# An instruction list laid out anew: attention and gated convolution FFN on one core, 852 entries, same work, another order

## The chip, the cores and the metric

The kernel runs on one core of one Trainium2 chip. The metric is device time in microseconds (us), the median of several executions. Before the change it is 177.59 us, over three runs that lie between 177.56 and 177.61 us.

## The reference

A linear attention without softmax is followed by a gated convolution network. Batch 8, 8 heads, 576 positions, head size 64, so 512 model columns; 1024 hidden columns.

```python
kv  = einsum('bhsd,bhse->bhde', k, v)
out = einsum('bhsd,bhde->bhse', q, kv)
x   = out / sqrt(mean(out*out, axis=-1) + 1e-6) * g_norm     # then (batch, 576, 512)
h   = maximum(x @ w_in, 0.0)                                 # 512 -> 1024
conv_out[s] = sum over k of conv_w[k] * h[s + k - 1]         # 3 taps along the positions
y   = (h * sigmoid(conv_out)) @ w_out                        # 1024 -> 512
```

## The kernel before

All inputs are read in float32 and turned into bf16 by the loads; the result goes back in float32. The eight batches are worked on in pairs for the last matmul, and otherwise one by one.

What each engine does, and when, is written in one string, `ORDER`. Each entry is a short name with its arguments, and a last loop at the end of the kernel calls one small function for each entry and then ties every engine's instructions to exactly the order in which they were issued. So the list is the schedule: an engine takes its instructions in the order of the list, and waits at the first one whose operands or target are not ready. Behind an `@` stands which of several equal buffers the entry writes: one of the eight banks of matmul results (two banks for entries that need a pair), one of the row buffers for output, one of the buffers for q, k, v, x, or one of the two sets of tap buffers. An entry that takes a buffer waits until everybody who read its previous content is done, a transfer out included.

The entries of which this text speaks, with the line of their work in the profile (arguments: batch, then half or tile):

- `Lq`, `Lk`, `Lv` (L347): load of q, k or v of one batch, issued by GpSimd (POOL).
- `qt` (L433) transposes q on TensorE, `qd` (L443, VectorE) copies it out. For batches 6 and 7 `tq` (L467) has the transfer engines transpose it, issued by SyncE (SP).
- `kv`, `kz` (L402, L479): k times v; `kvd` (L414, VectorE) or `kva` (L416, ScalarE) copies it out. `kx` (L489): a copy with halves swapped, by transfer.
- `ot`, `ox` (L460, L500): q times kv. `sq` (L509, ScalarE) squares it, `oc` (L521, ScalarE) copies it out.
- Normalisation, batches 0 to 3: `on` or `oq` (L528 with a full array, L537 with four 64-row pieces) sums the squares, `nl` (L545, ScalarE) takes the inverse root, `mo` (L556, VectorE) makes x.
- Normalisation, batches 4, 5 and 6, 7 together: `ss` (L566), `ln` (L574, ScalarE), `sl` (L581 to L584, four VectorE instructions), then `sp` (L593) spreads the result over the rows and `mu` (L599, VectorE) makes x.
- `hk`, `hs`, `hm` (L658, L628, L613): x times w_in; `rh`, `re` (L640, L619, ScalarE): the maximum with 0, which makes h.
- The convolution: `ta` (L681 and L682, VectorE) multiplies h by two of the taps, `aa` (L687) and `ab` (L692) add; `sg` (L698, ScalarE) is the sigmoid, `mg` (L722, VectorE) multiplies it into h.
- The last matmul: `om` (L732) in groups of four matmuls, two groups to a tile of 128 rows; the last tile in two halves, `oh` (L757). `ea` (L738, ScalarE) or `ed` (L743, VectorE) copies a tile out to a row buffer, `eh` (L767) or `dh` (L772) a half; `st` (L748) and `sh` (L777) store it, issued by SP.

ScalarE has two sets of functions, one for the inverse root and one for the sigmoid. A change from one to the other is an instruction of its own (L227, `ACT_TABLE_LOAD`), which `nl`, `ln`, `sc` and `sg` place when the other set is in.

Of the kernel before, what the change touches and what calls it, by code (L numbers as in the profile page):

```python
# [64 lines left out]
sq.0.1.1@3 oq.0.0.1@0 nl.0.0.1@2 fi.1.512@4 fi.1.512@4 hk.0.1.0.0@4 hk.0.1.0.1 rp.1.0@0 on.0.1.1@0 nl.0.1.1@3
hk.0.2.0.0@5 hk.0.2.0.1 rp.2.0 dg.3 mo.0.0.1 dg.2 hk.0.3.0.0@4 hk.0.3.0.1 hk.0.0.0.0@2 hk.0.0.0.1 rp.0.0 hk.0.0.1.0@3
rp.3.0 hk.0.1.1.0@5 hk.0.3.1.0@0 mo.0.1.1 hk.0.3.1.1 rp.3.1 hk.0.1.1.1 rp.1.1 hk.0.0.1.1 rp.0.1 dg.0 hk.0.2.1.0@1
hk.0.2.1.1 qt.1.0.0@6 kv.1.0.1@4 rp.2.1 cv.0.2@2 sc.0.2@0 cv.0.3@0 qd.1.0.0@2 kvd.1.0.1@1 ot.1.0.1@6 sc.0.3 pl
sq.1.0.1@4 cv.0.1@4 cv.0.0@2 Lq.1.2.2 Lk.1.2.2 Lv.1.2.2 sc.0.1@1 fi.2.512@0 qt.1.1.0@0 qd.1.1.0@3 mg.0.1.1 Lo.0.8
sc.0.0 mg.0.1.0 oq.1.0.1@4 nl.1.0.1@4 mo.1.0.1@1 fi.1.512@2 hk.0.5.1.0@2 hk.0.5.0.0@3 hk.0.5.0.1 rp.5.0 hk.0.5.1.1  # L70
rp.5.1 ta.0.1.5@0 hk.0.4.1.0@0 hk.0.4.1.1 rp.4.1 hk.0.7.0.0@1 hk.0.7.0.1 kv.1.1.1@4 kvd.1.1.1 rp.7.0 ot.1.0.0@2
sq.1.0.0@5 hk.0.7.1.0@6 hk.0.7.1.1 rp.7.1 ta.0.1.7@1 ot.1.1.1@0 sq.1.1.1@6 oq.1.0.0@4 nl.1.0.0@5 mo.1.0.0 hk.0.4.0.0@6
hk.0.4.0.1 rp.4.0 hk.0.6.1.0@7 hk.0.6.1.1 rp.6.1 oq.1.1.1@4 nl.1.1.1@6 mo.1.1.1 hk.0.6.0.0@6 Lq.2.0.4@2 hk.0.6.0.1
rp.6.0 ta.0.1.4 hk.1.6.1.0@7 ta.0.1.6 hk.1.0.1.0@2 ot.1.1.0@4 sq.1.1.0@7 aa.0.1.2 hk.1.1.1.0@3 hk.1.2.1.0@6 hk.1.6.1.1
# [5 lines left out]
Lq.3.0.4@0 Lk.3.0.4@0 Lv.3.0.4@1 Lq.4.0.4@1 aa.1.1.0 hk.1.4.0.0@3 om.0.1.0.4@2 rh.1.4.1 hk.1.4.0.1 rh.1.4.0  # L80
om.0.2.0.4@5 kv.2.0.2@6 mg.0.1.3 om.0.1.4.4 ab.1.1.0 sg.1.1.0 sg.1.1.1 kvd.2.0.2@2 ot.2.0.1@0 sq.2.0.1@0 ed.0.1@0
st.0.1 qt.3.1.0@6 qd.3.1.0@1 Lk.4.0.4@1 Lv.4.0.4@0 Lq.5.0.4@2 om.0.2.4.4 on.2.0.1@2 qt.3.0.0@6 qd.3.0.0@2 nl.2.0.1@8
mo.2.0.1@2 om.0.3.0.4@4 ea.0.2@1 ot.2.1.1@6 ot.2.1.0@2 mg.1.1.0 om.0.3.4.4 ed.0.3@2 sq.2.1.0@1 sq.2.1.1@2 on.2.1.0@0
nl.2.1.0@9 mo.2.1.0 om.0.0.0.4@5 hk.1.3.0.0@4 on.2.1.1@0 st.0.2 nl.2.1.1@0 mo.2.1.1 om.0.0.4.4 ed.0.0@3 ot.2.0.0@2
sq.2.0.0@3 hk.1.3.0.1 rh.1.3.0 st.0.0 kv.3.0.2@0 kvd.3.0.2@0 on.2.0.0@6 nl.2.0.0@1 mo.2.0.0 hs.2.0.1@4 rh.2.0.1@1
hs.2.5.1@5 rh.2.5.1 ot.3.1.1@0 sq.3.1.1@4 ta.1.1.5@1 ot.3.0.1@6 sq.3.0.1@5 hs.2.1.1@4 rh.2.1.1 hs.2.4.0@5 rh.2.4.0
ta.1.1.4 ta.1.1.2@0 pn hs.2.4.1@2 rh.2.4.1 hs.2.1.0@3 rh.2.1.0 on.3.1.1@4 nl.3.1.1@2 hs.2.2.0@2 rh.2.2.0 hs.2.5.0@3
rh.2.5.0 on.3.0.1@4 nl.3.0.1@3 aa.1.1.2 mo.3.1.1@0 hs.2.2.1@2 rh.2.2.1 hs.2.0.0@3 rh.2.0.0 ot.3.0.0@0 sq.3.0.0@6
mo.3.0.1 qt.4.0.0@4 qd.4.0.0@3 ta.1.1.3 ab.1.1.2 aa.1.1.1 ot.3.1.0@2 sq.3.1.0@7 hs.2.3.1@6 rh.2.3.1 on.3.0.0@4
nl.3.0.0@4 hs.3.4.1@7 rh.3.4.1 hs.3.1.1@6 rh.3.1.1 on.3.1.0@4 nl.3.1.0@5 mo.3.0.0 hs.3.6.1@7 rh.3.6.1 hs.2.6.0@6  # L90
mo.3.1.0 qt.5.0.0@4 qd.5.0.0@0 ab.1.1.1 qt.4.1.0@0 qd.4.1.0@4 sg.1.1.5 sg.1.1.4 Lq.6.0.4@0 mg.1.1.2 ta.1.1.6@1
ta.1.1.7 aa.1.1.3 hs.2.3.0@7 rh.2.3.0 hs.3.0.1@2 rh.3.0.1 rh.2.6.0 sg.1.1.3 sg.1.1.2 hs.3.7.0@3 hs.3.2.0@4 rh.3.2.0
hs.3.3.0@5 rh.3.3.0 rh.3.7.0 kv.4.0.2@0 kvd.4.0.2@1 hs.3.0.0@2 hs.3.3.1@6 mg.1.1.1 Lk.5.0.4@0 rh.3.3.1 hs.3.2.1@7
rh.3.2.1 hs.3.7.1@4 rh.3.7.1 hs.3.6.0@5 rh.3.6.0 rh.3.0.0 ab.1.1.3 ta.2.2.2@0 ta.2.2.3 hs.3.4.0@3 rh.3.4.0 sg.1.1.7
hs.3.1.0@4 hs.3.5.0@5 sg.1.1.6 rh.3.1.0 qt.5.1.0@0 qd.5.1.0@2 ot.4.0.0@6 sq.4.0.0@0 mg.1.1.3 rh.3.5.0 om.0.7.0.4@2
Lv.5.0.4@1 Lq.7.0.4@1 Lk.6.0.4@1 oc.4.0.0@6 hs.2.7.1@3 rh.2.7.1 ot.4.0.1@0 sq.4.0.1@1 oc.4.0.1@7 kv.5.0.2@4 ta.2.2.0@1
kvd.5.0.2@2 ot.4.1.0@6 oc.4.1.0@8 om.0.7.4.4 aa.2.2.1 ta.2.2.1 ed.0.7@4 aa.2.2.0 ot.5.0.0@4 sq.4.1.0@2 sq.5.0.0@3
oc.5.0.0@9 ot.5.0.1@0 sq.5.0.1@4 om.0.8.0.4@3 om.0.8.4.4 ed.0.8@5 ab.2.2.1 ot.5.1.1@6 oc.5.0.1@0 sq.5.1.1@5 ot.4.1.1@4
sq.4.1.1@6 oc.4.1.1@1 om.0.5.0.4@2 om.0.5.4.4 ed.0.5@0 ab.2.2.0 ot.5.1.0@0 om.0.4.0.4@3 ss.4.4.2@4 sq.5.1.0@7 ss.5.4.2
# [725 lines left out]
```

## Time and profile before

| | before |
|---|---|
| median time of three runs | 177.59 us (177.56 to 177.61) |
| span of the profiled execution, first to last instruction | 175.6 us |
| instructions | 5070 |
| TensorE matmul busy | 167.9 us (96%), 2097 recorded |
| VectorE busy | 149.5 us (85%) |
| ScalarE busy | 148.9 us (85%) |
| GpSimd busy | 22.2 us (13%) |
| granted TensorE clock | 1.000 |

No time of its own is recorded for the profiled execution; its span is 2.0 us under the median, and that is what lies around the span. On TensorE, instructions overlap: a matmul of 512 columns has a duration of 379 ns in the records while they start about 0.22 us apart. So TensorE's busy share says little, and the times from one start to the next are read instead. A few matmul records are missing (2097 of 2114 are there).

### The profile page before, as it was taken

How to read it: one execution, taken by the hardware profiler on the slowest of the kernel's cores; microseconds unless marked ns; L12 is line 12 of the kernel's file. 1: busy time of each engine (PE TensorE's matmuls, PEld its weight loads, DVE VectorE, ACT ScalarE, POOL GpSimd, SP SyncE). 2: the span in 40 equal slices, each digit the busy share in tenths (PEclk: the TensorE clock that was granted, in tenths of full speed). 3: DMA queues.
4: the chain of work that ended last, by engine and by line, in shares of the span. 5: the costliest groups of instructions: out<-in, count | busy, mean ns of one | idle time of the engine just before them, and what ended most of it. 6: DMA issues, size and time to landing. Idle time of an engine off the chain costs nothing.

```text
span 175.6 us, 5070 instructions
## 1 busy us (share of the span) xinstructions
PE 167.9 (96%) x2097; PEld 100.0 (57%) x2114; DVE 149.5 (85%) x290; ACT 148.9 (85%) x268; POOL 22.2 (13%) x35
## 2 busy tenths in 40 slices
PE   7979999999999999999999999999999999999992
PEld 2334766676447677644467764444877744444451
DVE  2796638899688899999999998989999999999950
ACT  2368899999978999999999998999999967676721
POOL 3094512200603013030000000000000000000000
PEclk9999999999999999999999999999999999999999
DMA  5999999999999999999999050330310003064486
GB/s 159 392 323 207 207 207 207 208 208 209 207 241 230 227 207 207 170 182 197 258 181 161 14 134 0 119 123 0 119 63 0 0 0 116 13 239 175 179 304 237
DMA packets 25911, 29.11 MB, mean 166 GB/s; under 512 B 6036, under 2 KB 20384, under 8 KB 25888
## 3 DMA queue, kind: packets, MB, share of 16 engines
q0 software_dynamic: 13296, 14.50, 49.2%
q1 hardware_dynamic: 12048, 13.11, 26.2%
q10 hardware_dynamic: 544, 1.18, 1.7%
q8 instruction: 16, 0.26, 0.6%
q14 instruction: 7, 0.06, 0.1%
HBM read 32.52 MB, written 9.44 MB: 239 GB/s over the span
## 4 chain that ended last, share of the span: by engine, by line
PE 76%; DVE 12%; ACT 5%; DMA 3%; issue 3%; ACTq 0%; DVEq 0%
PE banks L732 32%; PE banks L628 14%; PE banks L613 9%; PE banks L658 4%; DMA stg<-in_v_dram 3%; PE banks L460 3%; DVE h L722 2%; PE banks L708 2%; ACT taps L698 2%; PE banks L402 2%; PE banks L593 2%; PE banks L433 1%; PE banks L528 1%; DVE taps L681 1%; PE banks L286 1%
## 5 line engine op out<-in xcount | busy, mean ns | idle before, releaser
L732 PE MATMUL banks<-w_out_sb,h 128*128 128x512 bf16 x267 | 62.8, 379 | 1.2 <-issue 0.6
L698 ACT ACTIVATE taps<-taps,cw 128x576 bf16<-128x576 bf16 (+1 forms) x44 | 40.6, 958 | 5.7 <-DVE taps L692 5.5
L732 PEld LDWEIGHTS <-h 128*128 128x128 bf16 x280 | 26.2, 98 | 30.0 <-issue 1.1
L628 PE MATMUL banks<-x,w_in_sb 128*128 128x288 bf16 (+2 forms) x256 | 34.2, 286 | 0.0
L640 ACT ACTIVATE h<-banks 128x288 bf16<-128x288 f32 (+2 forms) x80 | 29.5, 460 | 0.3 <-PE banks L658 0.2
L628 PEld LDWEIGHTS <-w_in_sb 128*128 128x128 bf16 x256 | 24.4, 98 | 7.8 <-issue 0.8
L722 DVE TENSOR_TENSOR h<-h,taps 128x1152 bf16<-128x1152 bf16 (+1 forms) x24 | 22.8, 952 | 1.2 <-ACT taps L698 1.2
L687 DVE TENSOR_TENSOR taps<-taps 128x1152 bf16<-128x1152 bf16 (+1 forms) x22 | 21.5, 978 | 0.5
L509 ACT ACTIVATE sq<-banks 128x576 bf16<-128x576 f32 (+2 forms) x32 | 20.8, 691 | 1.1 <-PE banks L460 1.1
L692 DVE TENSOR_TENSOR taps<-taps,h 128x1152 bf16<-128x1152 bf16 (+1 forms) x22 | 21.4, 972 | 0.3
L681 DVE TENSOR_SCALAR taps<-h,cw 128x576 bf16<-128x576 bf16 (+1 forms) x44 | 18.7, 424 | 0.6 <-ACT h L665 0.5
L682 DVE TENSOR_SCALAR taps<-h,cw 128x576 bf16<-128x576 bf16 (+1 forms) x44 | 18.4, 418 | 0.0
L738 ACT ACTIVATE row<-banks 128x512 f32<-128x512 f32 x23 | 13.5, 597 | 5.7 <-PE banks L732 4.2
L658 PE MATMUL banks<-x,w_in_sb 128*128 128x288 bf16 (+2 forms) x128 | 17.7, 286 | 0.1
L613 PE MATMUL banks<-x,w_in_sb 128*128 128x288 bf16 x128 | 16.9, 286 | 0.0
L556 DVE SCALAR_TENSOR_TENSOR x<-banks,cw,rs 128x576 bf16<-128x576 f32 (+2 forms) x16 | 13.0, 816 | 3.9 <-ACT rs L545 3.6
L658 PEld LDWEIGHTS <-w_in_sb 128*128 128x128 bf16 x128 | 12.0, 98 | 4.4 <-issue 0.5
L227 ACT ACT_TABLE_LOAD x10 | 12.8, 1283 | 2.0 <-issue 1.8
L613 PEld LDWEIGHTS <-w_in_sb 128*128 128x128 bf16 x128 | 12.3, 98 | 3.7 <-issue 0.2
L443 DVE COPY qT<-banks 128x1152 bf16<-128x1152 bf16 (+2 forms) x13 | 8.8, 681 | 5.7 <-PE banks L433 5.7
L545 ACT ACTIVATE rs<-banks,eps_sb 128x576 f32<-128x576 f32 (+2 forms) x16 | 11.8, 740 | 1.1 <-PE banks L528 1.1
L599 DVE SCALAR_TENSOR_TENSOR x<-o,cw,banks 128x576 bf16<-128x576 f32 (+2 forms) x16 | 12.1, 810 | 0.7 <-PE banks L593 0.5
(89 smaller groups left out, 162.9 us busy)
## 6 DMA issues: line engine op xcount, KB each, us to landing
out_dram<-row SPq DMA_DIRECT2D x35, 256.0 KB, 2.3
q_sb<-in_q_dram POOLq DMA_DIRECT2D x6, 576.0 KB, 17.9
k_sb<-in_k_dram POOLq DMA_DIRECT2D x6, 576.0 KB, 14.5
v_sb<-in_v_dram POOLq DMA_DIRECT2D x6, 576.0 KB, 17.9
stg<-in_v_dram ACTq DMA_DIRECT2D x2, 576.0 KB, 6.2
stg<-in_k_dram SPq DMA_DIRECT2D x4, 288.0 KB, 6.9
w_in_sb<-in_moe_w_in_dram POOLq DMA_DIRECT2D x2, 512.0 KB, 9.9
w_out_sb<-in_moe_w_out_dram POOLq DMA_DIRECT2D x1, 1024.0 KB, 15.5
```

The lines of the kernel that those rows point to most:

```text
L509: nc.scalar.activation(T["sq", b, u, s], T["o", b, u, s], AX.Square)
L613: nc.tensor.matmul(ps[:, s, :HS], w_in_sb[:, t, f * P:(f + 1) * P], T["x", b][:, t, c0:c1], start=(t == 0), stop=(t == NT - 1))
L628: nc.tensor.matmul(ps, w_in_sb[:, t, f * P:(f + 1) * P], T["x", b][:, t, c0:c1], start=(t == 0), stop=(t == NT - 1))
L640: nc.scalar.activation(h, fr, AX.Relu)
L658: nc.tensor.matmul(T[at], w_in_sb[:, t, f * P:(f + 1) * P], T["x", b][:, t, c0:c1], start=(t == 0), stop=(t == NT - 1))
L681: nc.vector.tensor_scalar_mul(tap[:, 0, f % 2, :n, 8:8 + S], h[:, f], cw[:, f:f + 1])
L682: nc.vector.tensor_scalar_mul(tap[:, 1, f % 2, :n, :S], h[:, f], cw[:, 2 * NF + f:2 * NF + f + 1])
L687: nc.vector.tensor_add(tap[:, 1, :, :n, :S], tap[:, 0, :, :n, 7:7 + S], tap[:, 1, :, :n, 1:1 + S])
L692: nc.vector.tensor_add(y, y, span(b, n)[:, 2 * j:2 * j + 2])
L698: nc.scalar.activation(y, y, AX.Sigmoid, scale=cw[:, NF + f:NF + f + 1])
L722: nc.vector.tensor_mul(h, h, tap_of(b, j)[:, 1, :, :n, :S])
L732: nc.tensor.matmul(T["om", p, m], h[:, f, m * P:(m + 1) * P], w_out_sb[:, f, :], start=(f == 0), stop=(f == NF - 1))
```

## The change

The string `ORDER` is written anew. It has 852 entries before and after, and no function of the kernel changes. Nearly all entries are the same in another order; a few are exchanged for one that does the same on another engine or in another shape:

- `kvd.2.0.2` and `kvd.3.0.2` (VectorE) become `kva` (ScalarE);
- of the copies of output tiles, `ea.1.8`, `ea.3.1` and `ea.3.5` move to VectorE, `ed.2.8`, `ed.3.0`, `ed.3.2`, `ed.3.3` and `ed.3.4` to ScalarE, and the half tile `eh.3.8.0` to VectorE (`dh.3.8.0`);
- `oq.1.1.1` becomes `on.1.1.1`, so there are 2112 matmuls and no longer 2114.

Buffer numbers behind the `@` change as well. Entries of different engines stand in another order to each other from the first line on, but on the engines themselves the order is the same up to a point: TensorE's first difference is at its 453rd matmul, VectorE's at its 73rd instruction, ScalarE's at its 47th, GpSimd's when the load of batch 4 or 5 is reached. In the trace these are at 30 to 35 us.

The last lines of the list, before (two) and after (four):

```diff
-ed.3.7@4 om.3.5.4.4 ea.3.5@3 st.3.5 om.3.4.4.4 ed.3.4@5 st.3.4 st.3.7 om.3.6.4.4 ea.3.6@0 st.3.6 oh.3.8.1@1 eh.3.8.1@2
-sh.3.8.1 oh.3.8.0@0 eh.3.8.0@1 sh.3.8.0
+ab.7.1.2 ta.7.1.6@1 ta.7.1.7 aa.7.1.3 ab.7.1.3 om.3.2.0.4@1 sg.7.1.5 om.3.2.4.4 sg.7.1.4 ea.3.2@1 om.3.1.0.4@0
+om.3.1.4.4 ed.3.1@3 st.3.0 st.3.3 st.3.2 st.3.1 mg.7.1.2 om.3.6.0.4@1 sg.7.1.7 om.3.5.0.4@2 om.3.4.0.4@0 om.3.7.0.4@3
+sg.7.1.6 mg.7.1.3 om.3.4.4.4 om.3.7.4.4 ea.3.4@0 ed.3.7@1 st.3.7 om.3.5.4.4 ed.3.5@2 st.3.4 st.3.5 oh.3.8.0@0
+dh.3.8.0@3 sh.3.8.0 om.3.6.4.4 ea.3.6@4 st.3.6 oh.3.8.1@0 eh.3.8.1@0 sh.3.8.1
```

The first place is VectorE behind the `mg` of the first group of batch 1's convolution, in the trace the stretch from 42.5 to 54.3 us. `taps_72` and `taps_73` are the two tap buffers; L556 is `mo`, L443 is `qd`, L743 is `ed`, L414 is `kvd`. Before:

```order
L692 TENSOR_TENSOR taps_72<-taps_72,h 128x2x576
L414 CAST kvb<-banks 128x256
L743 COPY row<-banks 128x512
L443 COPY qT<-banks 128x1152 x2
L556 SCALAR_TENSOR_TENSOR x<-banks,cw,rs 128x2x288
L722 TENSOR_TENSOR h<-h,taps_72 128x2x576
L743 COPY row<-banks 128x512
L556 SCALAR_TENSOR_TENSOR x<-banks,cw,rs 128x2x288 x2
```

And now:

```order
L692 TENSOR_TENSOR taps_72<-taps_72,h 128x2x576
L681 TENSOR_SCALAR taps_73<-h,cw 128x576
L682 TENSOR_SCALAR taps_73<-h,cw 128x576
L681 TENSOR_SCALAR taps_73<-h,cw 128x576
L682 TENSOR_SCALAR taps_73<-h,cw 128x576
L743 COPY row<-banks 128x512
L443 COPY qT<-banks 128x1152
L687 TENSOR_TENSOR taps_73<-taps_73 128x2x576
L443 COPY qT<-banks 128x1152
L556 SCALAR_TENSOR_TENSOR x<-banks,cw,rs 128x2x288
L722 TENSOR_TENSOR h<-h,taps_72 128x2x576
```

The `kvd` has gone, and two `ta` and an `aa` of the next group have come in between the copies and the `mo`; an `ab` and two more `ta` follow behind the rows shown, again between `mo` instructions. Before, all of these stood behind the last `mo` of batch 2.

The second place is ScalarE around the first `ln` (L574), in the trace from 80.6 to 88.5 us: the last `sq` of batches 4 and 5 (L509), two changes of the function set (L227), the `oc` (L521), `ea` (L738), `sg` (L698) and `rh` (L640). Before:

```order
L509 ACTIVATE sq<-banks 128x2x288
L227 ACT_TABLE_LOAD
L574 ACTIVATE rs<-banks,eps_sb 128x320
L521 ACTIVATE o_1919<-banks 128x2x288
L521 ACTIVATE o_1921<-banks 128x2x288
L640 ACTIVATE h<-banks 128x288
L738 ACTIVATE row<-banks 128x512
L227 ACT_TABLE_LOAD
L698 ACTIVATE taps_72<-taps_72,cw 128x2x576
L738 ACTIVATE row<-banks 128x512
L640 ACTIVATE h<-banks 128x288 x2
```

And now:

```order
L640 ACTIVATE h<-banks 128x288
L521 ACTIVATE o_1866<-banks 128x2x288
L509 ACTIVATE sq<-banks 128x2x288 x3
L227 ACT_TABLE_LOAD
L574 ACTIVATE rs<-banks,eps_sb 128x320
L521 ACTIVATE o_1999<-banks 128x2x288
L521 ACTIVATE o_2009<-banks 128x2x288
L738 ACTIVATE row<-banks 128x512
L227 ACT_TABLE_LOAD
L698 ACTIVATE taps_72<-taps_72,cw 128x2x576
L738 ACTIVATE row<-banks 128x512
L640 ACTIVATE h<-banks 128x288 x2
```

The `rh` (`rh.2.7.0`) that stood between the two changes of the function set now stands ahead of both.

The third place is the end of SP's queue, the stores of the last tiles. The numbers are those of the row tiles; the last one, `row_3014` before and `row_3012` now, is the half tile that the kernel stores last. Before:

```order
L748 DMA out_0_dram<-row_2984 128x512
L748 DMA out_0_dram<-row_2971 128x512
L748 DMA out_0_dram<-row_2992 128x512
L777 DMA out_0_dram<-row_3003 128x256
L777 DMA out_0_dram<-row_3014 128x256
```

And now:

```order
L748 DMA out_0_dram<-row_2973 128x512
L748 DMA out_0_dram<-row_2982 128x512
L777 DMA out_0_dram<-row_2994 128x256
L748 DMA out_0_dram<-row_3001 128x512
L777 DMA out_0_dram<-row_3012 128x256
```

The first half tile is stored ahead of the last whole one. `row_2973` is `ea.3.4@0`, and the last half tile is `eh.3.8.1@0`: both lie in row buffer 0, so the copy of the last half tile now waits for the store of tile 3.4, which stands behind the store of tile 3.7 on SP.

More of the change, by code (lines that the diff above doesn't have):

```diff
@@ L65 @@
[L65 to L74, printed above, removed]
@@ L80 @@
[L80 to L89, printed above, removed]
@@ L90 @@
[L90 to L99, printed above, removed]
@@ new lines @@
+fi.4.512@1 gt.k.1.0 Li.0.4 pg cad.k.1.0 kv.0.0.1@4 Lq.1.0.2@1 pc Lk.1.0.2@0 kva.0.0.1@0 caa.q.1.0 ot.0.0.0@6
+fi.2.512@0 cad.v.3.0 Lv.1.0.2@1 sq.0.0.0@0 cad.k.2.0 qt.0.1.0@2 caa.v.2.0 Li.4.4 oq.0.0.0@4 fi.2.512@0 cad.k.3.0
+nl.0.0.0@0 qd.0.1.0@1 dg.1 kv.0.1.1@0 fi.2.512@2 Lq.1.2.2 cad.q.0.1 kva.0.1.1 Lk.1.2.2 ot.0.1.0@4 mo.0.0.0@0
+qt.0.0.1@2 fi.2.512@0 sq.0.1.0@1 Lv.1.2.2 cad.q.1.1 qa.0.0.1 oq.0.1.0@0 qt.0.1.1@6 nl.0.1.0@1 ot.0.0.1@2 qd.0.1.1
+sq.0.0.1@2 mo.0.1.0 ot.0.1.1@6 fi.1.512@0 sq.0.1.1@3 oq.0.0.1@0 fi.1.512@4 fi.1.512@4 dg.3 nl.0.0.1@2 hk.0.1.0.0@4
@@ new lines @@
+Lo.0.8 hk.0.1.0.1 mo.0.0.1 on.0.1.1@0 rp.1.0@0 hk.0.2.0.0@5 Lq.2.0.4@2 hk.0.2.0.1 nl.0.1.1@3 hk.0.3.0.0@4 dg.2
+hk.0.3.0.1 hk.0.0.0.0@2 rp.2.0 mo.0.1.1 hk.0.0.0.1 hk.0.0.1.0@3 rp.0.0 hk.0.1.1.0@5 Lk.2.0.4@1 rp.3.0 dg.0
+hk.0.3.1.0@0 hk.0.3.1.1 hk.0.1.1.1 rp.3.1 hk.0.0.1.1 hk.0.2.1.0@1 rp.1.1 Lv.2.0.4@0 hk.0.2.1.1 rp.0.1 qt.1.0.0@6
+rp.2.1 kv.1.0.1@4 qd.1.0.0@2 cv.0.2@2 kvd.1.0.1@1 pl cv.0.3@0 sc.0.2@0 ot.1.0.1@6 Lq.3.0.4@0 sc.0.3 cv.0.1@4
+sq.1.0.1@4 cv.0.0@2 fi.2.512@0 sc.0.1@1 sc.0.0 qt.1.1.0@0 oq.1.0.1@4 fi.1.512@2 qd.1.1.0@3 hk.0.5.1.0@2 hk.0.5.0.0@3
```

104 lines of the change are left out of this document (61 added, 43 removed).

## The prediction

> **What bounds the kernel now.** I read the page first, then the busy time by stretches, the chain of work that ended last, and the timeline where TensorE's starts lie further apart than its work. The page:
>
> ```profile
> span 175.6 us, 5070 instructions
> ## 1 busy us (share of the span) xinstructions
> PE 167.9 (96%) x2097; PEld 100.0 (57%) x2114; DVE 149.5 (85%) x290; ACT 148.9 (85%) x268; POOL 22.2 (13%) x35
> ```
>
> The busy time of each engine by stretches, cut where the program changes its work (convolution and attention of batches 1 to 3, up to the first `ln`, the first `sp`, and so on to the last `mg`):
>
> ```profile
> 33.00:55.00 22.00, 21.63 (x427) 13.71 (x429) 18.69 (x32) 19.82 (x39) 4.46 (x6) 1.00 1.20 218
> 55.00:81.00 26.00, 25.75 (x469) 16.83 (x470) 25.16 (x50) 25.90 (x56) 3.70 (x5) 1.00 1.23 199
> 81.00:91.00 10.00, 9.76 (x146) 5.24 (x147) 9.31 (x15) 9.94 (x16) 0.00 (x0) 1.00 1.25 234
> 91.00:114.00 23.00, 22.79 (x242) 14.67 (x246) 22.09 (x30) 22.51 (x36) 0.00 (x0) 1.00 0.47 86
> 114.00:123.00 9.00, 8.77 (x62) 3.73 (x63) 8.13 (x13) 8.94 (x12) 0.00 (x0) 1.00 0.16 60
> 123.00:141.00 18.00, 18.00 (x149) 14.04 (x148) 17.55 (x24) 17.86 (x37) 0.00 (x0) 1.00 0.12 45
> 141.00:166.70 25.70, 25.54 (x118) 11.59 (x119) 25.32 (x54) 17.92 (x31) 0.00 (x0) 1.00 0.33 123
> ```
>
> The columns are the stretch, its length, and busy time with count of TensorE, its weight loads, VectorE, ScalarE and GpSimd, then clock, transfer share and GB/s. TensorE is busy nearly throughout at full clock, and VectorE and ScalarE are close behind it; only VectorE from 33 to 55 us has much room, 3.3 us of 22. The end of the chain:
>
> ```profile
> 162.94 7.50 PE banks L732 x34
> 170.44 1.76 PE banks L757 x16
> 172.27 0.38 ACT row L767
> ```
>
> 34 matmuls of 512 columns in 7.50 us are 0.221 us each, with no room between them; 16 of half the width take 1.76. So from the first `om` of batches 4 and 5 the run is TensorE streaming to its last matmul, and then one copy, one store and the end. The list can't shorten that stream: both lists hold the same matmuls (but for `oq.1.1.1`, four small ones against two large). What can be won is the time in which TensorE waits. What can be lost has no such limit: any entry that comes late for TensorE is paid in full, as there is no idle time behind it in which to catch up.
>
> **The change part by part.** Up to about 33 us each engine's order is the old one, so nothing is won or lost there. After that I go from wait to wait.
>
> *The wait at `on.3.0.0`.* One row of the table of waits:
>
> ```profile
> PEld L528 <- DVE qT L443: 0.3, 1, 0.3
> ```
>
> TensorE waits 0.3 us for `qd.4.0.0`, whose source lies in the bank that `on.3.0.0` wants. In the new list the two still stand in this order on the same bank, but with one more small `ot` ahead on TensorE, and VectorE comes to the `qd` with less behind it. Won: between 0 and 0.3, I take 0.1.
>
> *The first `sp` and `mu`.* TensorE's timeline, start and duration first, each row a group of equal matmuls:
>
> ```profile
> 86.33 0.42 PE L593 MATMUL banks<-wparts,spread 32*128 32x288 bf16 x4
> 86.67 1.15 PE L628 MATMUL banks<-x,w_in_sb 128*128 128x288 bf16 x8
> 87.84 0.33 PE L500 MATMUL banks<-qT,kvb 64*64 64x320 bf16 x4
> 88.10 0.82 PE L593 MATMUL banks<-wparts,spread 32*128 32x288 bf16 x4
> ```
>
> Four `sp` matmuls take 0.42 when nothing holds them and 0.82 at 88.10: 0.40 of waiting. The eight of `hs` last 1.15 with the overlap of about 0.16 at their end (0.379 of duration against 0.221 from start to start), so `ox` could start at 87.66 and starts at 87.84: 0.18 more. Those at 88.10 want the banks of `hs.2.6.1` and `hs.3.5.1`, which ScalarE's `rh` empties late, since it comes from here:
>
> ```profile
> 84.01 0.42 ACT L640 ACTIVATE h<-banks 128x288 bf16<-128x288 f32 x1
> 84.30 0.62 ACT L738 ACTIVATE row<-banks 128x512 f32<-128x512 f32 x1
> 84.94 1.28 ACT L227 ACT_TABLE_LOAD   x1
> ```
>
> The first of these is `rh.2.7.0`, which the new list has moved ahead of `ln`. It goes from 84.01 to the next start at 84.30, so what follows it on ScalarE is 0.29 earlier, and the `rh` for which `sp` waits are too. Ahead of `ln` ScalarE pays the same 0.29, but there it had last waited for `ot.5.1.0`, which now comes two places sooner on TensorE. I take 0.3 of the 0.40 as won, and another 0.1 because `kvd.6` no longer stands between `sl` and a late `kz`: 0.4 in all. At best both waits go (0.6), at worst the early `rh` holds up `ln` by its 0.29 and nothing is won (a loss of 0.3).
>
> *The second `sp` and `mu`.* TensorE, and then VectorE at the `sl` ahead of it:
>
> ```profile
> 118.22 0.42 PE L593 MATMUL banks<-wparts,spread 32*128 32x256 bf16 x6
> 118.58 1.90 PE L732 MATMUL banks<-w_out_sb,h 128*128 128x512 bf16 x8
> 120.41 0.74 PE L593 MATMUL banks<-wparts,spread 32*128 32x320 bf16 x6
> ```
>
> ```profile
> 116.30 0.33 DVE L581 CAST hi<-rs 128x320 bf16<-128x320 f32 x1 [0.28 <-ACT rs L574]
> ```
>
> The same kind of group takes 0.42 and then 0.74: 0.32 of waiting for a `mu` to free a bank. The new list spreads these six `sp` over three places with half a tile of `om` between, where each bank's `mu` is one earlier; I count that two of three such waits go and one of about 0.2 stays. `sl` itself waits 0.28 for `ln`. ScalarE has one `ea` less ahead of it (0.48 from start to start), but VectorE has that copy more, 0.69 at most. These about cancel. Won: 0.1, between 0.5 won and 0.3 lost.
>
> A switch of the array between 128-row matmuls and smaller ones is not free: eight matmuls from 118.58 to 120.41 are 1.83, and 8 x 0.221 is 1.77, so 0.06 for the switch. The new list has 63 such switches from the first difference on, the old one 62, which changes the sum by 0.06 at most, and I leave it out. The Trainium skill, TensorEngine Tiling, section Key Properties, says that changing the tiling mode drains TensorE; by that the new list is dearer by one drain, and the trace agrees that there is one, and that it is small.
>
> *VectorE from 42 to 56 us.* Who VectorE waits for there, in total, times and longest, and some of its rows:
>
> ```profile
> DVE x L556 <- ACT rs L545: 1.5, 3, 0.7
> DVE qT L443 <- PE banks L433: 0.9, 1, 0.9
> DVE row L743 <- PE banks L732: 0.5, 1, 0.5
> ```
>
> ```profile
> 41.84 0.76 DVE L687 TENSOR_TENSOR taps<-taps 128x1152 bf16<-128x1152 bf16 x1
> 42.52 0.76 DVE L722 TENSOR_TENSOR h<-h,taps 128x1152 bf16<-128x1152 bf16 x1
> ...
> 54.33 0.82 DVE L556 SCALAR_TENSOR_TENSOR x<-banks,cw,rs 128x576 bf16<-128x576 f32 x1 [0.67 <-ACT rs L545]
> 55.06 0.36 DVE L681 TENSOR_SCALAR taps<-h,cw 128x576 bf16<-128x576 bf16 x1
> 55.34 0.36 DVE L682 TENSOR_SCALAR taps<-h,cw 128x576 bf16<-128x576 bf16 x1
> ```
>
> VectorE waits 2.9 us here. Into this the new list puts four `ta` (two instructions of 0.28 each, so 0.56) and an `aa` and an `ab` of 0.68 (from 41.84 to 42.52): 4 x 0.56 + 2 x 0.68 = 3.6 us. Out of it go two `kvd`, whose cost is bounded by the rows here as 0.28 to 0.68 each, say 0.7 together. So 3.6 us of work meet 2.9 + 0.7 = 3.6 us of room. It fits only if each piece falls into its own gap. Following the rows of the new list with these durations I find `mo.2.1.0` and `mo.2.1.1` about 0.25 later than before, with 0.15 to 0.2 of room at the matmuls that wait for their banks (`ot.2.0.0`, `on.2.0.0`). Lost: 0.1, and up to 1.2 where two pieces of 0.6 miss their gaps. What is won, VectorE being ahead by as much later, is worth nothing by itself, since TensorE sets the pace. ScalarE's two `kva` fall where it waited for `on`.
>
> *The end.* The store rows, and the last copies:
>
> ```profile
> DMA to landing us min/median/max: 2.0/2.3/7.8
> ```
>
> ```profile
> 171.35 0.38 ACT L767 ACTIVATE row<-banks 128x256 f32<-128x256 f32 x1 [0.28 <-DMA out_dram<-row]
> 171.76 1.25 SPq L777 DMA_DIRECT2D out_dram<-row  x2
> 172.27 0.38 ACT L767 ACTIVATE row<-banks 128x256 f32<-128x256 f32 x1 [0.54 <-PE banks L757]
> ```
>
> The last copy starts at 172.27, when its matmuls are done. In the new list it also needs row buffer 0 back, that is the landing of the store of tile 3.4. Counted back from 172.27 at 0.221 a matmul: behind tile 3.7 come four matmuls of 3.5, four of 3.6 and 16 halves, 8 x 0.221 + 1.76 = 3.5 us, so tile 3.7 is done at 168.7, its VectorE copy (0.69) at 169.4, and its store is issued then; that of 3.4 follows on SP about 0.4 later, at 169.8. With 2.3 us it lands at 172.1, with 2.7 at 172.5. So the last copy waits for 0 to 0.3 us, and everything behind it with it: lost 0.1. [...]
>
> The loads stand in almost the same order on GpSimd and are the same bytes. Up to the last load of batch 5 the same set has gone through, so `kv.5.0.2` finds its data when it did; v and k of batch 6 come one load earlier.
>
> **The sum.** Won 0.1 + 0.4 + 0.1 = 0.6, lost 0.1 + 0.1 = 0.2: 0.4 less. The span would be 175.2, and with the 2.0 us that lie around it the time is 177.2 (177.59 - 0.4). A measurement of this kernel can tell about 0.2%, 0.36 us, from no change, so this is only just outside.
>
> **The rivals.** *The waits only change their place.* The three gains rest on orders in which ScalarE, VectorE and TensorE hand each other banks with 0.1 to 0.2 us to spare, and a wait that goes at 88 us may return at 90 behind `mu.5`. For it speaks that ScalarE is 9.94 busy of 10 there; against it that the cause of the largest, `rh.2.7.0`, has clearly moved. Then 0.6 shrinks to 0.2, and with 0.2 lost the time is 177.6.
>
> *VectorE misses its gaps.* Between 42 and 56 us two inserted pieces of about 0.6 come ahead of `mo.2.1.0` and `mo.2.1.1` whose `nl` is done already. TensorE's next `ot` and `on` wait for the bank, ScalarE's `nl` waits for `on`, and the delay goes round once to the next `mo`. It decides at 0.15 us: a `mo.2.1.1` that ends later than that against TensorE's stream is paid. For it speaks 3.6 us of work in 3.6 of room; against it that in the new list the pieces do stand behind entries that waited. The price is up to 1.2 on the 177.2: 178.4. Half of it, with the worst of the first `ln` (0.3), gives the same side, 178.1.
>
> That the change doesn't do what it says is excluded by the order of the instructions; what its pricing is worth the rows can't say.
>
> **How the numbers follow.** The forecast, faster by over 0.2%, has 0.44: its gains have named causes. The waits that change their place, within 0.2%, have 0.23. Slower by over 0.2% has 0.33, nearly all the VectorE case, as three engines at 94 to 99% leave little to absorb an error. The gains can't exceed the waits: 0.3 + 0.58 + 0.32 + 0.28 are 1.5, so 176.1 is the floor; taking two thirds of it as the most that is likely, 1.0, the low end is 176.6. The high end is the VectorE case in full, 178.4. Under 2 in 10 lie outside.
>
> **What would show it.** Right: `ox.6.0.0` and the `sp` behind it follow `hs.3.5.1` within 0.3 us of waiting in all; ScalarE's second change of the function set starts 0.3 to 0.6 earlier than 84.94; TensorE's waits at the second `sp` are under 0.25; the last L767 copy waits for TensorE or by 0.1 for the store. Wrong: an `ot` or `on` between 50 and 55 us that waits over 0.2 for L556; a late `ln`; or the last L767 copy released by the store of L748 at 0.3 or more.

## The result, and the profile after

| | before | after |
|---|---|---|
| median of seven runs | 177.57 us (177.48 to 177.63) | 178.05 us (177.95 to 178.15) |
| span of the profiled execution | 175.6 us | 176.3 us |
| `hm.4.7` starts | 88.86 | 88.92 |
| `om.1.3` starts | 121.08 | 121.14 |
| `om.2.1` starts | 140.92 | 140.87 |
| last matmul starts | 171.91 | 172.02 |
| last copy (L767) starts | 172.27 | 173.02 |

The ratio is 1.0027 (95% interval 1.0017 to 1.0038): slower by 0.48 us, where 0.4 less was forecast; inside the range, on the wrong side. The two profiled spans lie further apart, by 0.78 before rounding: the new list was profiled in the slowest of its seven runs (178.15), and around the span the new list spends 1.75 to 1.85 us, the old one 1.90 to 2.01 (from the time and the span of every run on record).

The rows of the table from `hm.4.7` to the last matmul are entries ahead of which TensorE has done the same work in both lists (but for `oq.1.1.1`), so their difference is what the new list has lost or won up to there. 0.05 of each is there at 29 us already, ahead of the first changed instruction. So TensorE's stream is even within 0.1, and the loss lies behind its last matmul. The page:

```profile
span 176.3 us, 5070 instructions
PE 169.7 (96%) x2112; PEld 99.8 (57%) x2112; DVE 148.0 (84%) x287; ACT 150.2 (85%) x271; POOL 22.4 (13%) x35
```

The end: the chain's last row, then ScalarE's last copies, then SP's queue at the stores of tiles 3.7 and 3.4, and the waits on SP and at the end:

```profile
170.44 2.48 DMA out_dram<-row
```

```profile
168.04 0.60 ACT L738 ACTIVATE row<-banks 128x512 f32<-128x512 f32 x1 [2.84 <-issue]
171.46 0.60 ACT L738 ACTIVATE row<-banks 128x512 f32<-128x512 f32 x1 [2.82 <-PE banks L732]
173.02 0.38 ACT L767 ACTIVATE row<-banks 128x256 f32<-128x256 f32 x1 [0.96 <-DMA out_dram<-row]
```

```profile
169.58 0.33 SPq L748 DMA_DIRECT2D out_dram<-row  x1
...
170.44 0.33 SPq L748 DMA_DIRECT2D out_dram<-row  x1
```

Before, the chain ended in 16 half matmuls and the last copy waited for them. Now it ends in a store. Tile 3.4 is copied out by 168.64, but its store stands on SP behind that of 3.7, which goes out at 169.58, and follows only at 170.44. It lands 2.48 later, at 172.91, and the last copy, whose matmuls were done for it at about 172.37 (in the run below with the store moved it starts then), starts at 173.02: 0.65 lost. A last copy that the store releases with 0.3 or more of waiting is a sign of being wrong that the prediction had named.

On the way TensorE's waits changed their place. At the normalisation of batch 3, `on` (L528):

```profile
60.78 0.42 PE L528 MATMUL banks<-sq,ones 128*128 128x288 bf16 x2
61.04 1.14 PE L628 MATMUL banks<-x,w_in_sb 128*128 128x288 bf16 x8
62.25 0.41 PE L528 MATMUL banks<-sq,ones 128*128 128x288 bf16 x2
62.55 1.14 PE L628 MATMUL banks<-x,w_in_sb 128*128 128x288 bf16 x8
```

The idle time ahead of the weights of `on.3.0.0` is 0.16 instead of 0.34, still ended by VectorE's `qd.4.0.0`. But the eight `hs` matmuls from 61.04 are done at 62.02 (8 x 0.122), and `on.3.1.0` starts only at 62.25: it takes the bank of `on.3.0.0`, which ScalarE's `nl` reads until 62.20. In the old list the matmuls behind it started at 62.50, here at 62.55: nothing won.

The first `sp` and `mu`, and what comes ahead of them, TensorE:

```profile
73.69 0.40 PE L460 MATMUL banks<-qT,kvb 64*64 64x288 bf16 x4
73.99 0.77 PE L402 MATMUL banks<-v_sb,k_sb 64*64 64x64 bf16 x72
74.83 0.32 PE L460 MATMUL banks<-qT,kvb 64*64 64x288 bf16 x4
75.08 1.04 PE L732 MATMUL banks<-w_out_sb,h 128*128 128x512 bf16 x4
...
85.42 0.30 PE L593 MATMUL banks<-wparts,spread 32*128 32x288 bf16 x4
85.65 1.04 PE L732 MATMUL banks<-w_out_sb,h 128*128 128x512 bf16 x4
86.62 0.38 PE L593 MATMUL banks<-wparts,spread 32*128 32x288 bf16 x4
86.93 1.15 PE L628 MATMUL banks<-x,w_in_sb 128*128 128x288 bf16 x8
88.16 0.33 PE L500 MATMUL banks<-qT,kvb 64*64 64x320 bf16 x4
88.42 0.57 PE L593 MATMUL banks<-wparts,spread 32*128 32x288 bf16 x4
88.92 1.15 PE L613 MATMUL banks<-x,w_in_sb 128*128 128x288 bf16 x8
90.00 0.42 PE L593 MATMUL banks<-wparts,spread 32*128 32x288 bf16 x4
```

The four groups of `sp` take 0.30 + 0.38 + 0.57 + 0.42 = 1.67 instead of 2.08 (0.42, 0.42, 0.82, 0.42): the 0.4 that the prediction looked for is won here. But TensorE comes to them later, since it has waited more before. One such place is the `ot` and `kv` at 74 us: the stretch from 73.69 to 75.08 is 1.39, and in the old list 1.13, from 73.62 to 74.75 (the recorded start of the `om` behind it less one matmul of 0.22 that is missing in the records), by these rows of before:

```profile
73.62 0.32 PE L460 MATMUL banks<-qT,kvb 64*64 64x288 bf16 x4
73.77 0.92 PE L402 MATMUL banks<-v_sb,k_sb 64*64 64x64 bf16 x72
74.50 0.31 PE L460 MATMUL banks<-qT,kvb 64*64 64x288 bf16 x4
74.97 0.81 PE L732 MATMUL banks<-w_out_sb,h 128*128 128x512 bf16 x3 [0.16 <-issue]
```

And ScalarE's `ln` starts at 82.89 instead of 82.53. Its second change of the function set starts at 85.00 instead of 84.94, where the prediction looked for 0.3 to 0.6 earlier. So `hm.4.7` is where it was. ScalarE had no room to give, as the busy times of the new list by stretches show (ScalarE's is the fourth of the five engines):

```profile
72.00:76.00 4.00, 3.93 (x95) 2.21 (x93) 4.00 (x10) 4.00 (x11) 0.91 (x1) 1.00 0.89 152
76.00:82.00 6.00, 6.00 (x58) 2.64 (x58) 5.80 (x7) 5.98 (x12) 0.76 (x2) 1.00 1.19 225
82.00:86.00 4.00, 4.00 (x90) 1.88 (x90) 3.68 (x8) 3.97 (x6) 0.00 (x0) 1.00 1.19 237
```

### The profile page after: what moved, and what is told of

The parts are those of the page before. It is cut to its first block, busy times and chain, and to the rows that moved or that the text cites. A ratio compares the mean times of both kernels' runs of the same rounds, so it can differ in the third digit from the quotient of the medians.

```text
span 176.3 us, 5070 instructions
## 1 busy us (share of the span) xinstructions
PE 169.7 (96%) x2112; PEld 99.8 (57%) x2112; DVE 148.0 (84%) x287; ACT 150.2 (85%) x271; POOL 22.4 (13%) x35
## 4 chain that ended last, share of the span: by engine, by line
PE 79%; DVE 9%; ACT 5%; DMA 4%; issue 2%; SPq 0%; ACTq 0%; DVEq 0%
PE banks L732 33%; PE banks L628 13%; PE banks L613 9%; PE banks L658 8%; DMA stg<-in_v_dram 3%; PE banks L460 3%; PE banks L286 2%; PE banks L433 2%; PE banks L708 2%; PE banks L528 2%; DVE h L722 2%; PE banks L402 1%; DMA out_dram<-row 1%; DVE x L599 1%; PE banks L593 1%
## 5 line engine op out<-in xcount | busy, mean ns | idle before, releaser
L732 PE MATMUL banks<-w_out_sb,h 128*128 128x512 bf16 x280 | 64.8, 380 | 0.0
L698 ACT ACTIVATE taps<-taps,cw 128x576 bf16<-128x576 bf16 (+1 forms) x44 | 40.4, 965 | 2.3 <-DVE taps L692 2.1
L640 ACT ACTIVATE h<-banks 128x288 bf16<-128x288 f32 (+2 forms) x80 | 30.0, 487 | 0.5 <-PE banks L658 0.5
L738 ACT ACTIVATE row<-banks 128x512 f32<-128x512 f32 x25 | 14.9, 597 | 8.3 <-PE banks L732 4.8
L509 ACT ACTIVATE sq<-banks 128x576 bf16<-128x576 f32 (+2 forms) x32 | 20.8, 700 | 1.1 <-PE banks L460 0.9
L556 DVE SCALAR_TENSOR_TENSOR x<-banks,cw,rs 128x576 bf16<-128x576 f32 (+2 forms) x16 | 13.0, 814 | 5.3 <-ACT rs L545 5.0
L286 PE MATMUL banks<-zero 128*128 128x512 bf16 x37 | 11.9, 446 | 1.2 <-DVE zero L265 1.2
L443 DVE COPY qT<-banks 128x1152 bf16<-128x1152 bf16 (+2 forms) x13 | 8.7, 680 | 5.1 <-PE banks L433 4.8
```

Source lines behind the costliest of these rows:

```text
L509: nc.scalar.activation(T["sq", b, u, s], T["o", b, u, s], AX.Square)
L640: nc.scalar.activation(h, fr, AX.Relu)
L698: nc.scalar.activation(y, y, AX.Sigmoid, scale=cw[:, NF + f:NF + f + 1])
L732: nc.tensor.matmul(T["om", p, m], h[:, f, m * P:(m + 1) * P], w_out_sb[:, f, :], start=(f == 0), stop=(f == NF - 1))
```

## The experiments

Times in this section stand beside runs of the old list on the same chip. The tail means the last 18 entries of a list; "the store of tile 3.4" is `st.3.4`. The first four changes ask whether it is the tail.

**The old tail behind the new list.** Both lists have done the same work at their 834th entry, so the tails can be exchanged; the bank numbers are set to those that are free there.

```diff
-om.3.4.4.4 om.3.7.4.4 ea.3.4@0 ed.3.7@1 st.3.7 om.3.5.4.4 ed.3.5@2 st.3.4 st.3.5 oh.3.8.0@0 ...
+om.3.7.4.4 ed.3.7@4 om.3.5.4.4 ea.3.5@3 st.3.5 om.3.4.4.4 ed.3.4@5 st.3.4 st.3.7 om.3.6.4.4 ...
```

> The new list up to its 834th entry, and the old list's last 18 entries behind it (both lists have done the same entries there). Theory 1, the tail: in the profiled execution of the new list the last copy (L767) waits 0.96 us for the store of tile 3.4, of which 0.65 lies behind the end of the last matmul's work; TensorE's stream as a whole is only 0.1 later than in the old list. Without that tail the time is 177.4 to 177.6, and the last copy waits for TensorE. Rival, the stream: the new list loses its 0.5 on the way and the tail only takes up time that would pass anyway; then it stays at 178.0, with the last matmul 0.4 or more later than in the old list.

Measured 177.54 (177.41 to 177.68), beside 177.68 for the old list: ratio 0.9992 (0.9983 to 1.0001). The last copy waits for TensorE:

```profile
172.34 0.38 ACT L767 ACTIVATE row<-banks 128x256 f32<-128x256 f32 x1 [0.54 <-PE banks L757]
```

The new list's stream costs nothing against the old one; the loss is the tail's.

**The new tail behind the old list.**

> The other half of the exchange: the old list up to its 834th entry, the new list's last 18 entries behind it. Theory 1, the tail: 0.4 to 0.65 slower than the old list, 178.0 to 178.2, with the last copy waiting for the store of tile 3.4. Rival, the stream: within 0.15 of the old list, 177.6 to 177.7.

Measured 180.35, far outside both answers, and it says nothing about the tail: the row buffers of the new tail are those of late stores of the old list, and the copy of tile 3.4 waited 3.43 us for one. With fitted row buffers (`ea.3.4@3 ed.3.7@4 ed.3.5@5 dh.3.8.0@0 ea.3.6@2 eh.3.8.1@3`):

> The old list up to its 834th entry and the new list's last 18 behind it, as in the run that gave 180.35, but with row buffers that fit the old list's stores: there the copy of tile 3.4 waited 3.43 us for a store of the old part. The last half tile still takes the row buffer of tile 3.4. Theory, the tail costs by itself: 0.35 to 0.6 slower than the old list, 177.95 to 178.2. Rival: the tail costs only behind the new list; within 0.15 of the old list.

Measured 177.99 (177.83 to 178.23), beside 177.76, ratio 1.0000 (0.9985 to 1.0015): by time this is unclear, since the old list itself spread from 177.41 to 178.76 on that chip; it does not decide by itself. The profile shows the theory's mechanism, a span of 176.0 and this row for the last copy:

```profile
172.97 0.38 ACT L767 ACTIVATE row<-banks 128x256 f32<-128x256 f32 x1 [1.02 <-DMA out_dram<-row]
```

**The store of tile 3.4 first.**

```diff
-ea.3.4@0 ed.3.7@1 st.3.7 om.3.5.4.4 ed.3.5@2 st.3.4 st.3.5
+ea.3.4@0 st.3.4 ed.3.7@1 st.3.7 om.3.5.4.4 ed.3.5@2 st.3.5
```

> The new list with one entry moved: the store of tile 3.4 directly behind its copy, ahead of the store of tile 3.7; the row buffers stay. Theory 1: the store is issued at about 168.7 instead of 170.4 and lands by 171.0, so the last copy waits for TensorE and the time falls by 0.4 to 0.65, to 177.4 to 177.65. In the profiled run of the new list SP stood 0.46 us ahead of that store with everything done that it waits for, and in the old list 0.45 ahead of another store; both times it was SP's 80th recorded instruction. If it is a matter of the place in SP's code, the same 0.45 stands here ahead of whatever is SP's 80th instruction, without harm. Rival: SP's delay goes with that store, or writing a row buffer twice at the end costs in itself; then less than 0.2 is won.

Measured 177.37 (177.28 to 177.54), beside 177.68: ratio 0.9983 (0.9974 to 0.9991). One entry moved takes the whole loss away. SP's store of tile 3.4, the last copy, and the time from issue to landing of the stores issued from 169 us on:

```profile
168.66 0.33 SPq L748 DMA_DIRECT2D out_dram<-row  x1
```

```profile
172.37 0.38 ACT L767 ACTIVATE row<-banks 128x256 f32<-128x256 f32 x1 [0.33 <-PE banks L757]
```

```profile
DMA to landing us min/median/max: 1.8/2.2/2.4
```

**A free row buffer for the last copy.** `eh.3.8.1@0` becomes `eh.3.8.1@5`, nothing else.

> The new list with one number changed: the last half tile goes to row buffer 5, which has been free for long, instead of 0; the order of the stores stays. Theory 1: the last copy waits for TensorE alone; 177.4 to 177.65, the same as with the store moved. Rival, the stream: 178.0.

Measured 178.11 (178.02 to 178.33), ratio 1.0023 (1.0014 to 1.0032). Theory 1 as it was put falls here: the last copy is released by TensorE, as it said, and yet nothing is won. The copy, and the time to landing of the stores issued from 169 us on:

```profile
172.53 0.38 ACT L767 ACTIVATE row<-banks 128x256 f32<-128x256 f32 x1 [0.28 <-PE banks L757]
```

```profile
DMA to landing us min/median/max: 2.2/2.7/3.1
```

Its last store is issued at 172.94 and lands at 175.56; in the new list 173.43 and 175.38. (This execution is 0.2 later from 29 us on.) So two things end together in the new list: the late last copy, and the drain, the time until the stores already issued have all landed. Four whole tiles and two halves go out within 3.2 us, and they land up to 3.1 us after their issue, where with the store moved it is 2.4 at most. Take away the one, and the other sets the end. Moving one store forward takes away both.

The next two ask what makes the drain long; the one behind them asks about SP, and bears on the drain as well.

**The halves last**, as in the old list, row buffer 5:

```diff
-ed.3.5@2 st.3.4 st.3.5 oh.3.8.0@0 dh.3.8.0@3 sh.3.8.0 om.3.6.4.4 ea.3.6@4 st.3.6 oh.3.8.1@0 ...
+ed.3.5@2 st.3.4 st.3.5 om.3.6.4.4 ea.3.6@4 st.3.6 oh.3.8.0@0 dh.3.8.0@3 sh.3.8.0 oh.3.8.1@5 ...
```

> The new list with the last copy in row buffer 5, as in the run with a free row (178.11), and besides both half tiles behind tile 3.6, as in the old list. That run showed that the last copy alone is not it: its copy waits for TensorE (172.53), and still the last store lands at 175.56, 0.9 later than in the run with the old tail, though both issue three whole and two half tiles from 170.4 to 170.6 on. Theory A, the order of the stores: a half tile of 1 KB rows ahead of a whole one holds the drain up; with the halves last the time is 177.5 to 177.7. Theory B, the lateness: what counts is that three whole and two half tiles are still to be written at 170.6, or what else uses the transfer engines then; it stays at 178.0 to 178.2.

Measured 178.13 (178.09 to 178.24), beside 177.61: ratio 1.0029 (1.0018 to 1.0040). The order of the stores is not it.

**The first half on ScalarE**: `dh.3.8.0@3` becomes `eh.3.8.0@3`, with the free row buffer.

> The run with a free row (178.11) with one entry exchanged: the first half tile is copied by ScalarE (eh) and no longer by VectorE (dh); the order of the stores stays whole, whole, whole, half, whole, half. In that run an 8 KB instruction transfer of 0.31 us starts at 173.16, in the middle of the drain, and the 16 parts of a store land up to 1.05 us apart behind it; with the old tail that transfer starts at 176.79, behind the end, and they land within 0.43. Theory C, the instruction transfer: with one VectorE instruction less it moves behind the end, the spread of a store's parts stays under 0.6 and the time falls to 177.6 to 177.9. Theory A (order of the stores) and B (lateness): 178.0 to 178.2.

Measured 177.89 (177.57 to 177.98), ratio 1.0013 (1.0004 to 1.0022), against 1.0023 with `dh`. The intervals overlap, so the rows have to carry this. The second 8 KB instruction transfer starts at 177.05, and stores land sooner:

```profile
DMA to landing us min/median/max: 2.0/2.5/2.7
```

The parts of a store lie 0.55 to 0.64 us apart from the second store on, where theory C had said under 0.6. Counted from the same `ot` at 29 us, the last store lands 0.36 earlier than in the run with a free row, and still 0.39 later than with the store moved. So about half of the loss is gone, and the other half, 0.28 by time, stays. Lateness itself (theory B) would explain it. But another 8 KB instruction transfer, at 171.18, still lies in this drain, and the second run below speaks for that one.

**SP's code moved.** Stores of early tiles in two halves of 64 rows each, one store in the first run, three in the second (shown here), on the new list as it is:

```diff
-nc.sync.dma_start(out=out_rows[at:at + P, :], in_=T["os", p, m])
+for a in ((0, 64), (64, 128)) if (p, m) in ((0, 1), (0, 2), (0, 7)) else ((0, 128),):
+    nc.sync.dma_start(out=out_rows[at + a[0]:at + a[1], :], in_=T["os", p, m][a[0]:a[1]])
```

> The new list as it is, but the store of tile 0.1, at about 50 us, is made in two halves of 64 rows, so that every later instruction of SP's stands one or two places further back in its code. Theory, SP's place in its code: the 0.45 us in which SP stands still with nothing to wait for stays at its 80th recorded instruction, which is now the store of tile 3.7 or the wait before it, where SP waits for VectorE anyway; the store of tile 3.4 is issued at about 170.0 instead of 170.44, and the time falls by 0.2 to 0.5, to 177.6 to 177.85. Rival: the delay belongs to the store of tile 3.4, or to the pace of two stores behind each other; 178.0 to 178.1, with 0.45 in the same place.

Measured 178.09 (177.96 to 178.21), ratio 1.0027 (1.0017 to 1.0036): no change, and an edit that was too small. It put one instruction in and not two, so that SP's 80th was the wait ahead of the same store: it stood 0.455 us there, and the store went out at 170.43 as before. That the stop stays at the 80th while the code moves is what the theory says; the time told nothing.

> The new list as it is, but the stores of tiles 0.1, 0.2 and 0.7, all before 90 us, are made in two halves each, which puts SP's later instructions three places further back (one split moved them by one, and the 0.45 us stood still at the 80th, now the wait ahead of the store of tile 3.4). Theory, SP's place in its code: the 80th instruction is now the wait ahead of the store of tile 3.7, at about 164.8, where SP has 4.8 us to spare. The store of tile 3.4 is issued at 169.95 to 170.0 and no longer at 170.44, the last copy waits 0.2 us or less for it, and the time falls to 177.55 to 177.85. Rival: the lateness of the whole drain counts and not SP's 0.45; 178.0 to 178.1.

Now SP's 80th instruction comes at 165.43, 0.448 late, where SP has time. The store of tile 3.4 follows that of 3.7 by 0.43 and no longer by 0.86, and the last copy waits less:

```profile
169.83 0.33 SPq L748 DMA_DIRECT2D out_dram<-row  x1
...
170.26 0.38 SPq L748 DMA_DIRECT2D out_dram<-row  x1
```

```profile
172.67 0.38 ACT L767 ACTIVATE row<-banks 128x256 f32<-128x256 f32 x1 [0.36 <-DMA out_dram<-row]
```

The last store lands at 174.80 instead of 175.38, in an execution that is 0.2 later from 29 us on: counted from there 0.76 earlier, and as early as with the store moved, within 0.02. Both 8 KB instruction transfers lie outside this drain (166.26 and 176.62), the parts of a store are at most 0.21 us apart, and the stores land 1.7 to 2.5 us after their issue, though the last two are issued as late as in the run with a free row. So the lateness of the last stores alone does not make the drain long; transfers of instructions among the stores fit better. That is not separated from the second to fourth store, which go out 0.2 to 0.35 earlier than there.

Yet the span is 176.3 again. The time is 177.91 (177.80 to 178.11), beside 177.76: ratio 0.9997 (0.9981 to 1.0012), an interval that the spread of the old list on this chip makes wide, and some 0.15 under the new list's 178.05 on another chip. From the last landing to the end it is 1.50 us here, and 0.96 before and after: SP asks for the stores' semaphores in a fixed order, 0.065 apart, and the last store's stands third of nine here, where it stood last but one (0.3 of the 0.54); and VectorE stopped for 0.46 in its closing instructions, for which the others waited (0.2). SP's stop and what it does to the last copy and the stores are shown; its price in the time is not.

The last three are about TensorE's stream, on the new list with the store moved (177.37).

**`rh.2.7.0` back behind `ln`**, with its `hs`:

```diff
-hs.2.7.0@1 ... rh.2.7.0 oc.4.1.1@5 ... ss.5.4.2 ln.4@0 aa.2.2.1
+... oc.4.1.1@5 ... ss.5.4.2 hs.2.7.0@5 ln.4@0 rh.2.7.0 aa.2.2.1
```

> The new list with the store of tile 3.4 first (177.37), and besides hs.2.7.0 and rh.2.7.0 put back behind ss.5.4.2 and ln.4, about where the old list has them. The prediction's step: rh.2.7.0 ahead of ln wins 0.3 of TensorE's waiting at the first sp and mu, so this loses 0.3: 177.7. Rival: ScalarE is full from 72 to 86 us in both lists, rh.2.6.1 starts at 87.87 and 87.94 and hm.4.7 at 88.86 and 88.92, so the move of a piece within a full engine wins nothing, and ln comes 0.3 earlier here; 177.2 to 177.4, with hm.4.7 within 0.15 of 88.9.

Measured 177.90 (177.83 to 177.97), beside 177.61, so 0.5 lost against the list it was made from (177.37, on another chip): more than the prediction's step, but not by that step. `hm.4.7` comes 0.43 later, counted from the same `ot` at 29 us, so the rival's time falls too; only `ln` comes as the rival had it, at 82.51, 0.3 earlier counted from there. What was lost is on TensorE:

```profile
PE banks L460 <- ACT sq L509: 0.5, 1, 0.5
```

`hs.2.7.0` had filled 0.5 us ahead of `ot.5.0.1`, whose bank waits for `sq.4.1.0`; now TensorE stands there. The edit moved two things (and gave the `hs` another bank), so it says what the `hs` is worth in its place, and little on the `rh`.

**`oc.4.0.0` ahead of `rh.3.7.1`**, on ScalarE at 74 us:

```diff
-rh.3.5.0 rh.3.1.0 rh.3.7.1 oc.4.0.0@0
+rh.3.5.0 rh.3.1.0 oc.4.0.0@0 rh.3.7.1
```

> The new list with the store of tile 3.4 first (177.37), and one more entry moved: rh.3.7.1 from ahead of oc.4.0.0 to behind it on ScalarE. In the profiled run of the new list oc.4.0.0 ends at 74.79, and ot.4.1.0, which takes over its bank, starts at 74.83 after 0.26 of waiting; in the old list oc.4.0.0 ends at 74.42 and ot.4.1.0 starts at 74.50. Theory: what the new list won at the first sp it had lost here, because three rh stand ahead of oc.4.0.0; with one of them behind it ot.4.1.0 starts 0.25 earlier, hm.4.7 by 0.15 to 0.25 (88.70 instead of 88.92), and the time is 177.1 to 177.25. Rival: ScalarE is full up to 91 us, so the 0.26 only becomes a later wait; hm.4.7 stays at 88.9 and the time at 177.3 to 177.4.

Measured 177.52 (177.31 to 178.06), beside 177.76. In its profile `hm.4.7` and the last matmul come 0.2 later than in the list it was made from, but so does an `ot` at 29 us, ahead of the change: nothing won and nothing lost. TensorE:

```profile
73.90 0.68 PE L460 MATMUL banks<-qT,kvb 64*64 64x288 bf16 x4
74.39 0.80 PE L402 MATMUL banks<-v_sb,k_sb 64*64 64x64 bf16 x72
75.00 0.31 PE L460 MATMUL banks<-qT,kvb 64*64 64x288 bf16 x4
75.25 0.60 PE L732 MATMUL banks<-w_out_sb,h 128*128 128x512 bf16 x2
```

The wait at the second `ot` is gone and a longer one stands at the first (0.68 instead of 0.40): 1.35 in all instead of 1.39. That one comes behind the first matmul of `ot.4.0.1`, and the profile doesn't name what it waits for. It isn't the list's: in executions with the same order up to there the second matmul starts 0.08 (new list) to 0.48 us (SP's code moved, second run) behind the first. In the next run, whose list is the same as here up to 140 us, these rows take only 1.13, as in the old list, and `hm.4.7` comes 0.04 earlier and no more. So the rival holds by these rows, though its time, 177.3 to 177.4, was missed too.

**Other banks for `om.2.8` and `om.2.4`**, besides that: `om.2.8.0.4@7 om.2.4.0.4@4` for `@2` and `@1`.

> As the run with rh.3.7.1 moved, and besides om.2.8 and om.2.4 take banks 7 and 4, free for longer, and no longer 2 and 1. In the new list TensorE waits 0.17 at om.2.8.0.4 (143.63) for the bank that rh.7.7.0 empties. Theory, TensorE's stream sets the end: another 0.1 to 0.17 is won, 176.95 to 177.1. Rival: VectorE, which is 24.5 of 25.7 us busy from 141 us on, sets when the last mg are done, and the 0.17 comes back as a wait behind it; the same time as without the change of banks.

Measured 177.38 (177.12 to 177.69), 0.14 under the run before on the same chip, with ranges that overlap; the theory's 176.95 to 177.1 had counted on a gain of the run before that didn't come. TensorE at 143 us in the new list, and here:

```profile
142.81 1.19 PE L732 MATMUL banks<-w_out_sb,h 128*128 128x512 bf16 x4
```

```profile
142.79 1.46 PE L732 MATMUL banks<-w_out_sb,h 128*128 128x512 bf16 x6
```

Six in 1.46 leave no gap (5 x 0.216 + 0.38); four in 1.19 hold one of 0.16. Counted from the same `ot` at 29 us, the last matmul comes 0.18 earlier than in the list with the store moved, and the last landing 0.17 earlier. So TensorE's stream sets the end once the tail is mended. This list is faster than the old one: ratio 0.9964 (0.9948 to 0.9979).

## Why the prediction was wrong, step by step

**The tail** was named, with its cause, and mis-sized: 0.1 taken, 0.65 measured. The step that failed is "that of 3.4 follows on SP about 0.4 later, at 169.8": it followed after 0.86, at 170.44. The prediction has the store land at 172.1, and it landed at 172.91. Of this 0.8, SP's stop is 0.46; 0.18 came ahead of it (the store of tile 3.7 went out at 169.58 and not at 169.4), and 0.18 behind it (2.48 from issue to landing and not 2.3). SP stopped at its 80th recorded instruction, which in the old list is harmless, since that place lies ahead of a store that has to wait for VectorE anyway. Besides, the sum had no term for the drain: with four whole tiles and two halves held back to the last 3 us, the stores' landing alone gives the same end. What makes that landing slow is shown in part only.

**`on.3.0.0`**: 0.1 taken, nothing won. Its wait shrank by 0.18, and `on.3.1.0`, which takes over its bank, got one of 0.23.

**The first `sp` and `mu`**: 0.4 taken, and 0.4 won in those rows, but none at `hm.4.7`. The failed step is the one on ScalarE: "what follows it on ScalarE is 0.29 earlier". ScalarE is full from 72 us on, so a piece moved forward only trades places: `ln` came 0.36 later, and `rh.2.6.1` at 87.94 instead of 87.87. That ScalarE waited for `ot.5.1.0` ahead of `ln` was an assumption; no row had shown it. (A slip without weight: the overlap of 0.16 was worked out with rows of 512 columns. Those of `hs` have 288, last 0.286 and start 0.122 apart, which gives 0.16 as well.)

**The second `sp` and `mu`**: 0.1 taken, nothing won up to `om.1.3`; a wait of 0.11 at `hs.6.4.1` has gone later on, and one of 0.16 at `om.2.8` has come.

**VectorE from 42 to 56 us** was worked out rightly, and its price was too high. `mo.2.1.0` and `mo.2.1.1` are later by 0.32 and 0.26, where about 0.25 was said:

```profile
50.78 0.81 DVE L556 SCALAR_TENSOR_TENSOR x<-banks,cw,rs 128x576 bf16<-128x576 f32 x1
...
52.07 0.81 DVE L556 SCALAR_TENSOR_TENSOR x<-banks,cw,rs 128x576 bf16<-128x576 f32 x1
```

Before, they started at 50.46 and 51.81. TensorE covered it: `ot.2.0.0` starts at 51.87 instead of 51.80, `on.2.0.0` at 52.98 instead of 53.10. The rival that put the slower side here had the wrong place, and that the measured 178.05 lies close to its 178.1 is chance.

So on TensorE's stream the rival of the waits that only change their place came true, and the slower side came from the tail. The list with the store moved is 0.31 faster than the old one by time, though both profiled spans are 175.6. Over all their runs, its spans are 0.13 shorter on average, and the rest lies around the span (1.80 us instead of 1.94); why that differs stays open. What TensorE waits for at 74 us, behind the first matmul of `ot.4.0.1`, is open too.

## What to carry to other kernels

A wait that goes is won only if the engine that makes it wait has room; on an engine without idle time, look for the next entry that comes as much later, and compare where both lists have done the same work, not the wait itself. At the end of a kernel, count the bytes that are still to be stored when the last results come, and let no finished tile stand behind an unfinished one in a queue that works in order. A mended wait should be tried alone: here the late copy and the late drain ended together, and taking away the one that the profile named (the copy's wait) changed nothing.

## What the runs showed of the hardware

SP stops for about 0.45 us ahead of its 80th recorded instruction, with everything done that it waits for: 0.438 to 0.464 in nine profiles, whatever stands there, and in the others a wait of that length covers it. In these nine an 8 KB transfer on an instruction queue starts 0.73 to 0.87 after the 80th. That the stop is one of fetching instructions is inferred from this and from its place in the code; no row names a cause. The Trainium skill, Runtime: NRT & Kernel Launch, section Instruction fetch mechanics, says that instructions come in blocks of 256, and that crossing into the next block is mostly hidden. If this place is such a crossing, the trace shows 0.45 that is not hidden.

A store comes in 16 parts, and instruction transfers of 8 KB among the last stores go with parts that land far apart. With two such transfers in the drain of the new tail they lie up to 1.05 to 1.09 us apart (new list, free row, halves last, one store split); with one, up to 0.64 and 0.73 (first half on ScalarE, new tail with fitted buffers); with none, up to 0.21 (three stores split). It is no rule: two transfers lie among the last stores of the list with the store moved as well, and there the parts are at most 0.55 apart, in the lists made from it 0.47 to 1.06.

The time around the span is no constant: 1.90 to 2.01 us in the runs of the old list, 1.75 to 1.85 in those of the new one, 1.88 to 1.99 with the first half on ScalarE.
